# Global/local attention, MoE and soft MoE on one core: two H pieces of tile 1 taken from beside attention of batch 0 to beside the joint softmax chain of tiles 2 and 0

## The chip, the cores and the metric

The kernel runs on one core of one Trainium2 chip. The metric is device time in microseconds (us) of one execution; times below are medians of several runs unless a single execution is named.

## What is computed

The reference, cut to its structure (4 batches, 8 heads, 512 local and 32 global positions, head width 64; model width 512, hidden width 2048; 8 soft-MoE experts with 4 slots each):

```
out_l = softmax([q_l k_g^T, band(q_l k_l^T, 32)] / 8) [v_g; v_l]     per batch and head
out_g = softmax(q_g [k_g; k_l]^T / 8) [v_g; v_l]
x = concat(out_g, out_l)                     rows x 512
h = x @ w_in;  g = max(0.01 h, h);  y = g @ w_out
logits = y @ phi;  d = softmax over rows;  c = softmax over slots
slot_in = d^T y;  slot_out = per expert relu(slot_in w1) w2
result = c @ slot_out
```

w_in and w_out come as 64-bit words and are turned into float32 on the chip.

## The kernel before

The local rows are cut into 16 row tiles of 128 (tile t is part t % 4 of batch t // 4); tile 16 holds the global rows. The kernel works through attention batch by batch and head pair by head pair, and through the row tiles beside it.

**Attention of one head pair n.** T_ (L390 to L406) transposes keys and queries on TensorE, ScalarE evicts them (L394), VectorE builds key windows `kw` (L405, L406). a_S forms scores `sc` on TensorE (L434), VectorE adds the mask and takes the maximum (L446), ScalarE takes the exponentials `se` (L454). a_E transposes them (L473), a_V multiplies by the values `vw` (`po`, L493) and VectorE scales the product (L501). g_S, g_E and g_V do the same for the 32 global queries (`gl` L519, `gs` L536, `get` L561, `gpo` L579, `gxt` L592).

**A row tile t.** b_X transposes the tile and splits it into a high and a low part (`xxh`, `xxl`; tile 2 uses the buffers `qn`, `kn` of the attention and is named `xqn`, `xkn`). b_H(t, f), here called H(t,f), is one of four pieces: 12 matmuls of 512 columns into `hp` (L689) and one Prelu on ScalarE (L696), for hidden columns 512 f to 512 f + 511. A tile needs all four. b_L transposes the hidden tile (`gtp`, L726; copies L728), p_M multiplies by `pmat` to logits `lg` (L887), and p_D1 to p_D3 and u_add run the column softmax and the weighted sum `up` (L810). Tiles 2 and 0 go through this joint softmax chain as one pair, then tiles 1 and 3 (pair_items).

**w_out.** p_items takes w_out in 16 chunks of 128 rows, c0 to c15 here. Each is loaded (`rraw` and, for the first ones, `sraw`, `eraw`, `kraw`, L233), converted by two ScalarE instructions (L251, L250), two on VectorE (L253, L257) and one on GpSimd (L261), stored to DRAM as `wo_f` (L338), transposed on TensorE (`wotp`, L345), evicted by ScalarE (L347) and multiplied with phi (`ptps`, L354). Three `wo` buffers and a ring of four raw buffers tie the chunks to each other: chunk k+3 overwrites the buffer of chunk k, and the load of chunk k+4 waits until GpSimd has ended chunk k. All loads and stores named here are issued in order by SyncE's one queue.

**Order of the work.** The program writes work items with a weight each, `merge` interleaves two lists in proportion to their weights, and a scheduler then fixes the order on each engine, which the chip follows. So one order per engine is fixed before the run.

Before the change, H(0..2, f) run in the order tile 0, 1, 2 for each f: f = 0 and 1 beside the conversion of w_in, f = 2 and 3 beside the first w_out chunks. Then the attention of batch 1 and the other chunks follow with H(3,0), H(3,1), and then the pair chains.

Of the kernel before, what the change touches and what calls it, by code (L numbers as in the profile page):

```python
# [20 lines left out]
def kernel(  # L21
# [24 lines left out]
    NQ = FF // 512  # L46
# [18 lines left out]
    def hb(name):  # L65
        return bank("hb", name, 2)
# [550 lines left out]
    def load_ahead(n):  # L617
        if n < len(order):
            load_qk(*order[n])
# [8 lines left out]
    def step(n):  # L628

        b, i = order[n]  # L630
        last = i == NP - 1
        e = (0.9, lambda: a_E(b, i))
        v = (1.6, lambda: (a_V(b, i), None if n < NP else load_vn(b) if i == NP - 2 else load_v(n + (1 if last else 2))))
        ns = [(2.7, lambda: a_S(*order[n + 1]))] if n + 1 < NN else []
        nt = [(0.9, lambda: T_(n + 2))] if n + 2 < NN else []
        if not last:
            gs = [(2.2, lambda: g_S(b))] if i == NP - 2 else []
            return ns + [e] + gs + nt + [v]
        gv = (2.1, lambda: (g_V(b), load_v(n + 2) if b else None))
        return [e, (0, lambda: None), v, (1.1, lambda: g_E(b))] + ns + nt + [gv]  # L640
# [33 lines left out]
    def b_H(t, f, half=None):  # L674
        xh, xl = xt[t]
        if half != 1:
            if f == 0:
                gt[t] = (
                    xa.tile([P, FF], F32, tag="xn", name="gx", bufs=1) if t in (3, NTT - 1)
                    else sa.tile([P, FF], F32, tag="vw", name="g2", bufs=2) if t == 2  # L680
                    else sb.tile([P, FF], F32, tag="g", name="g", bufs=2)
                )
            hps[0] = hb("hp")
        hp = hps[0]
        w = wi[f]
        lo, hi = {None: (0, KD), 0: (0, KD // 2), 1: (KD // 2, KD)}[half]
        for k in range(lo, hi):
            for n, (a, c) in enumerate(((xh, 0), (xh, 1), (xl, 0))):
                nc.tensor.matmul(  # L689
                    hp, a[:, k, :], w[c][:, k, :],  # L690
                    start=(k == 0 and n == 0), stop=(k == KD - 1 and n == 2),
                )
        if half == 0:
            return
        gs = gt[t][:, 512 * f:512 * f + 512]
        nc.scalar.activation(out=gs, in_=hp, func=AF.Prelu, alpha=0.01)  # L696
        if t in BLK or t in HALF and f < 2:
            blocks(t, f, gs)
# [3 lines left out]
    def blocks(t, f, gs):  # L702

        if f % 2 == 0:
            gbl[0] = sb.tile([P, 2, 512], F32, tag="gT", name="gb", bufs=2)
            gbl[1] = gp[0].tile([P, 2, 4, P], F32, tag="g8", name="g8", bufs=2)
        gb, g8 = gbl[0], gbl[1]
        nc.vector.transpose(out=gb[:, f % 2], in_=gs)  # L708
        lst[t, f] = g8[:, f % 2]
        if f % 2 == 0:  # L710
            return
        src = gb.rearrange("p f (q c j) -> p (f q) c j", c=4, j=32)
        dst = g8.rearrange("p f q (a j) -> p (f q) a j", j=32)
        for n in range(16):
            a, c = n // 4, (n + n // 4) % 4
            copy = {"P": nc.gpsimd.tensor_copy, "A": nc.scalar.copy, "D": nc.vector.tensor_copy}[MOVE[f // 2][n]]
            copy(dst[32 * c:32 * c + 32, :, a], src[32 * a:32 * a + 32, :, c])  # L717
# [3 lines left out]
    def b_L(t, f, ev=None):  # L721
        g = gt[t]
        pt = tp("gtp")
        for c in range(4):
            o = 512 * f + P * c
            nc.tensor.transpose(pt[:, P * c:P * c + P], g[:, o:o + P], ident)  # L726
        gT = part("gT")
        (ev or (nc.vector.tensor_copy if f % 2 and not (t >= 6 and f in (1, 3, 9)) else nc.scalar.copy))(  # L728
            gT, pt
        )  # L730
        lst[t, f] = gT.rearrange("p (c t) -> p c t", c=4)
# [71 lines left out]
    def u_add(ds, last):  # L803

        up = bank("po", "up", 1) if last >= 7 else hb("up")
        later = "u" in ms
        ms["u"] = True
        for n, (d, g) in enumerate(ds):
            for j in range(4):
                ms["up"] = nc.tensor.matmul(  # L810
                    up[32 * j:32 * j + 32, :], d, g[:, 512 * j:512 * j + 512],
                    start=(n == 0), stop=(n == len(ds) - 1), skip_group_check=True,
                ).ins
        if later:
            nc.vector.scalar_tensor_tensor(
                out=uacc, in0=uacc, scalar=ms["al"], in1=up, op0=ALU.mult, op1=ALU.add
            )
        else:
            nc.vector.tensor_copy(uacc, up)
# [59 lines left out]
    def p_M(ts, i):  # L879

        if i == 0:
            ms["M"] = bank("sm", "lg", 1)
        lg = ms["M"]
        for f in range(NQ):
            gT = lst.pop((ts[i], f))
            for c in range(4):
                nc.tensor.matmul(  # L887
                    lg[32 * c:32 * c + 32, P * i:P * i + P], pmat[:, c, f, :], gT[:, c, :],
                    start=(f == 0), stop=(f == NQ - 1), skip_group_check=True,
                )  # L890

    def p_D1(ts):
        lp = sb.tile([P, 2 * P], F32, tag="lp", name="lp", bufs=1)
        nc.vector.tensor_copy(lp, ms["M"][:, 0:2 * P])
        ms["lp"] = lp

    def p_D2(ts):
        ms["st"] = d_cols(ms["M"][:, 2 * P:4 * P], ms["lp"])

    def p_D3(ts):  # L900
        lg = ms["M"]
        for i, t in enumerate(ts):
            nc.tensor.transpose(lg[:, P * i:P * i + P], ms["st"][:, P * i:P * i + P], ident)
        ms["ds"] = [(d_rows(t, lg[:, P * i:P * i + 64]), gt.pop(t)) for i, t in enumerate(ts)]

    def pair_items(ts):
        its = []
        for i, t in enumerate(ts):
            its += [
                (0.9, lambda t=t: (b_L(t, 0), b_L(t, 1))),  # L910
                (0.9, lambda t=t: (b_L(t, 2), b_L(t, 3))),
                (0.6, lambda i=i: p_M(ts, i)),
            ]
        return its + [
            (0.1, lambda: p_D1(ts)),
            (0.5, lambda: p_D2(ts)),
            (0.5, lambda: p_D3(ts)),
            (2.0, lambda: u_add(ms["ds"], ts[-1])),
        ]
# [36 lines left out]
    def merge(a, c):  # L956
        ta, tb = sum(x[0] for x in a) or 1.0, sum(x[0] for x in c) or 1.0
        pa = pb = 0.0
        a, c = list(a), list(c)
        while a or c:  # L960
            if a and (not c or pa / ta <= pb / tb):
                w, f = a.pop(0)[:2]
                pa += w
            else:
                w, f = c.pop(0)[:2]
                pb += w
            f()
# [6 lines left out]
    t = wp.tile([P, 4, NT, 2, D], F32, tag="w", name="qk")  # L974
# [36 lines left out]
        conv(4)  # L1011
    load_ahead(NP)
    load_ahead(NP + 1)
    hs = [[(2.6, lambda t=t, f=f: b_H(t, f)) for t in range(3)] for f in range(NQ)]
    with tc.issue_after(exp_last[0]):
        conv(4)
        merge(hs[1], wit[:4])
# [8 lines left out]
    s4, s5, s6, s7 = (step(n) for n in range(NP, 2 * NP))  # L1026
    h3 = [(2.6, lambda f=f: b_H(3, f)) for f in range(NQ)]
# [4 lines left out]
    xb.append(bctx.enter_context(tc.tile_pool(name="xb", bufs=1, side="right")))  # L1032
    gctx = ExitStack()
    gp.append(gctx.enter_context(tc.tile_pool(name="gp", bufs=1, side="right")))
    merge(pair_items((2, 0)), [h3[2]] + s5[:1])
    load_v(NP + 1)
    merge(h3[3:] + pair_items((1, 3)), s4[-1:] + s5[1:] + s6 + s7)
    b_X(NT)
# [342 lines left out]
```

## Time and profile before

| | us |
|---|---|
| median of 3 runs | 499.89 |
| lowest, highest run | 499.71, 501.77 |
| the profiled execution | 496.2 |
| span of that execution, first to last instruction | 494.5 |
| TensorE busy in the span | 463.5 (94%) |
| VectorE, ScalarE, GpSimd busy | 275.0, 234.3, 160.3 |
| granted TensorE clock, mean | 0.979 |

Busy time of TensorE contains the tail of each matmul, so matmuls that wait one after the other for small results still look nearly dense. All times of the trace are counted from the first instruction of the span; the stretch around the change is 85 to 185 us.

### The profile page before, as it was taken

How to read it: one execution, taken by the hardware profiler on the slowest of the kernel's cores; microseconds unless marked ns; L12 is line 12 of the kernel's file. 1: busy time of each engine (PE TensorE's matmuls, PEld its weight loads, DVE VectorE, ACT ScalarE, POOL GpSimd, SP SyncE). 2: the span in 40 equal slices, each digit the busy share in tenths (PEclk: the TensorE clock that was granted, in tenths of full speed). 3: DMA queues.
4: the chain of work that ended last, by engine and by line, in shares of the span. 5: the costliest groups of instructions: out<-in, count | busy, mean ns of one | idle time of the engine just before them, and what ended most of it. 6: DMA issues, size and time to landing. Idle time of an engine off the chain costs nothing.

```text
span 494.5 us, 13438 instructions
## 1 busy us (share of the span) xinstructions
PE 463.5 (94%) x5323; PEld 322.0 (65%) x5323; DVE 275.0 (56%) x886; ACT 234.3 (47%) x680; POOL 160.3 (32%) x281
## 2 busy tenths in 40 slices
PE   7867889999989999999999999999999999999993
PEld 5645668666766657776777676777777777533463
DVE  4585888498547776556554656427666511413332
ACT  4776899588655345543435444234444432201122
POOL 2044887342400113460615243243667700000000
PEclk9986899999999999999999999999999999999998
DMA  9989598599457655334250231169420079999977
GB/s 177 223 200 267 183 292 313 185 304 311 150 143 144 143 118 93 85 76 129 60 106 1 60 60 45 44 220 405 150 78 2 23 266 357 364 397 371 305 237 214
DMA packets 118362, 90.23 MB, mean 182 GB/s; under 512 B 75356, under 2 KB 100764, under 8 KB 118300
## 3 DMA queue, kind: packets, MB, share of 16 engines
q1 hardware_dynamic: 115628, 88.33, 61.8%
q10 hardware_dynamic: 2672, 1.05, 0.8%
q8 instruction: 42, 0.69, 0.6%
q14 instruction: 20, 0.16, 0.1%
HBM read 76.68 MB, written 8.65 MB: 173 GB/s over the span
## 4 chain that ended last, share of the span: by engine, by line
PE 78%; DVE 4%; ACT 4%; DMA 1%; issue 1%; POOL 0%; ACTq 0%; DVEq 0%; POOLq 0%
PE hp L689 38%; PE gtp L726 4%; PE ehp L1221 3%; PE sc L434 3%; PE up L810 3%; PE po L493 3%; PE lg L740 2%; PE etp L473 2%; PE sop L1297 2%; PE sop L1275 1%; PE gpo L579 1%; PE wotp L345 1%; PE qTp L390 1%; PE kTp L390 1%; PE xtp L659 1%; PE gl L519 1%
## 5 line engine op out<-in xcount | busy, mean ns | idle before, releaser
L689 PE MATMUL hp<-wi,xxh 128*128 128x512 f32 x512 | 167.2, 408 | 1.2 <-ACT xxh L665 1.2
L689 PEld LDWEIGHTS hp<-wi,xxh 128*128 128x128 f32 x512 | 91.8, 190 | 28.2 <-issue 8.2
L717 POOL COPY g<-gb 32x256 f32<-32x256 f32 x206 | 82.7, 401 | 82.6 <-DVE gb L708 55.5
L689 PE MATMUL hp<-wi,xxl 128*128 128x512 f32 x256 | 101.0, 396 | 0.0
L696 ACT ACTIVATE g<-hp 128x512 f32<-128x512 f32 x60 | 35.3, 595 | 56.2 <-PE hp L689 54.2
L454 ACT ACTIVATE se<-se,nmx 128x128 f32<-128x128 f32 x128 | 49.6, 390 | 21.5 <-DVE nmx L452 21.4
L689 PEld LDWEIGHTS hp<-wi,xxl 128*128 128x128 f32 x256 | 48.3, 189 | 12.5 <-issue 1.7
L200 POOL COPY vw<-vw 32x1664 f32<-32x1664 f32 x10 | 15.8, 1575 | 78.3 <-DMA vw<-in_v_g_dram 34.9
L446 DVE CUSTOM_DVE_ANT_0 se<-sc,mask 128x128 f32<-128x128 f32 x128 | 28.9, 284 | 12.1 <-PE sc L434 12.0
L261 POOL TENSOR_TENSOR wn<-wn,rraw 128x512 int32<-128x512 int32 x16 | 22.8, 1435 | 34.5 <-DVE wn L257 33.0
L708 DVE STREAM_TRANSPOSE gb<-g 128x512 f32<-128x512 f32 x32 | 22.2, 702 | 19.3 <-ACT g L696 14.0
L434 PE MATMUL sc<-kw,qT 64*32 64x128 f32 x1024 | 29.2, 283 | 0.8 <-DVE mx L446 0.4
L493 PE MATMUL po<-vw,eT 128*32 128x64 f32 x1024 | 24.2, 232 | 3.5 <-issue 2.1
L261 POOL TENSOR_TENSOR wo<-wo,rraw 128x512 int32<-128x512 int32 x12 | 16.0, 1332 | 31.7 <-DVE wo L257 7.2
L434 PEld LDWEIGHTS sc<-kw,qT 64*32 64x32 f32 x1024 | 19.8, 109 | 8.9 <-issue 5.3
L493 PEld LDWEIGHTS po<-vw,eT 128*32 128x32 f32 x1024 | 18.4, 116 | 10.2 <-issue 7.4
L477 DVE COPY eT<-etp 128x512 f32<-128x512 f32 x28 | 18.7, 684 | 9.9 <-PE etp L473 9.9
L454 ACT ACTIVATION_READ_ACCUMULATOR se<-se,nmx 128x1 f32 x128 | 24.1, 188 | 0.0
L473 PE MATMUL etp<-identr,se 128*128 128x128 f32 x128 | 22.4, 296 | 0.2
L405 DVE COPY kw<-kT 128x672 f32<-128x672 f32 x32 | 19.8, 653 | 3.1 <-ACT kT L394 2.7
L251 ACT ACTIVATE rraw<-rraw 128x512 int32<-128x512 uint32 x28 | 18.7, 673 | 4.3 <-DMA rraw<-in_moe_w_out_dram 3.1
L473 PEld LDWEIGHTS etp<-identr,se 128*128 128x128 f32 x128 | 15.8, 146 | 6.3 <-ACT se L454 2.3
(232 smaller groups left out, 777.9 us busy)
## 6 DMA issues: line engine op xcount, KB each, us to landing
ew<-in_moe_w_dram SPq DMA_DIRECT2D x23, 1024.0 KB, 9.5
rraw<-in_moe_w_in_dram SPq DMA_DIRECT2D x16, 512.0 KB, 5.5
vw<-in_v_l_dram SPq DMA_DIRECT2D x60, 112.0 KB, 3.2
rraw<-in_moe_w_out_dram SPq DMA_DIRECT2D x12, 512.0 KB, 6.7
ew<-in_moe_w_dram SPq DMA_DIRECT2D x9, 512.0 KB, 9.2
ew<-in_moe_w_dram SPq DMA_DIRECT2D x17, 256.0 KB, 5.5
wo_f<-wo SPq DMA_DIRECT2D x16, 256.0 KB, 3.2
vn<-in_v_l_dram SPq DMA_DIRECT2D x4, 1024.0 KB, 6.3
```

The lines of the kernel that those rows point to most:

```text
L261: nc.gpsimd.tensor_tensor(out=di, in0=di, in1=m, op=ALU.add)
L405: nc.vector.tensor_copy(kw[:, :, 0:96], src)
L434: last_a[0] = nc.tensor.matmul(bks[e][32 * u:32 * u + 32, P * T:P * T + P], qt[64 * e:64 * e + 64, 32 * U:32 * U + 32], kw[win(U) // (NW / ...
L446: nc.vector.tensor_tensor_reduce(out=s[:, T, :], in0=bk[:, P * T:P * T + P], in1=mask[:, 0 if T == 0 else 2 if T == NT - 1 else 1, :], sca ...
L454: exp_last[0] = nc.scalar.activation(out=s[:, T, :], in_=s[:, T, :], func=AF.Exp, bias=nmx[:, e, T:T + 1], accum_out=sm[:, T, e:e + 1],).ins
L473: last_a[0] = nc.tensor.transpose(pt[:, P * T:P * T + P], es[e][:, T, :], ident).ins
L493: last_a[0] = nc.tensor.matmul(pov[32 * u:32 * u + 32, T, e, :], ets[e][:, 32 * U:32 * U + 32], vw[:, win(U), e, :], start=True, stop=True ...
L689: nc.tensor.matmul(hp, a[:, k, :], w[c][:, k, :], start=(k == 0 and n == 0), stop=(k == KD - 1 and n == 2),)
L696: nc.scalar.activation(out=gs, in_=hp, func=AF.Prelu, alpha=0.01)
L708: nc.vector.transpose(out=gb[:, f % 2], in_=gs)
L717: copy(dst[32 * c:32 * c + 32, :, a], src[32 * a:32 * a + 32, :, c])
L726: nc.tensor.transpose(pt[:, P * c:P * c + P], g[:, o:o + P], ident)
```

## The change

For f = 2 and 3 only tiles 2 and 0 stay in the first list, tile 2 first. H(1,2) and H(1,3) form a new list `h1`, which is put with H(3,2) and one item of head pair 5 beside pair_items((2, 0)).

```
-    hs = [[(2.6, lambda t=t, f=f: b_H(t, f)) for t in range(3)] for f in range(NQ)]
+    hs = [[(2.6, lambda t=t, f=f: b_H(t, f)) for t in ((0, 1, 2) if f < 2 else (2, 0))] for f in range(NQ)]
+    h1 = [(2.6, lambda f=f: b_H(1, f)) for f in range(2, NQ)]
...
-    merge(pair_items((2, 0)), [h3[2]] + s5[:1])
+    merge(pair_items((2, 0)), h1[:1] + s5[:1] + h1[1:] + [h3[2]])
```

No instruction is added or taken away. What the scheduler makes of it on the engines is shown at three places.

TensorE from the transposes of chunk c1 on, after the first 11 matmuls of H(0,3); names are as above. Before:

```order
L345 MATMUL wotp<-identr,wo 128x128 x4
L354 MATMUL ptps<-wt,phis 32x128
L519 MATMUL gl<-kT,qgT 32x512 x4
L689 MATMUL hp<-wi,xxl 128x512
L689 MATMUL hp<-wi,xxh 128x512 x2
L689 MATMUL hp<-wi,xxl 128x512
```

And with the change:

```order
L345 MATMUL wotp<-identr,wo 128x128 x4
L354 MATMUL ptps<-wt,phis 32x128
L519 MATMUL gl<-kT,qgT 32x512 x4
L689 MATMUL hp<-wi,xxl 128x512
L345 MATMUL wotp<-identr,wo 128x128 x4
L354 MATMUL ptps<-wt,phis 32x128
L345 MATMUL wotp<-identr,wo 128x128 x4
L354 MATMUL ptps<-wt,phis 32x128
L519 MATMUL gl<-kT,qgT 32x512 x4
L561 MATMUL get<-identr,gs 128x128 x4
```

Before, the 24 matmuls of H(1,3) and H(2,3) follow, with c2 and c3 after 12 of them each; now c2 and c3 follow at once, and no H piece comes until H(3,0).

SyncE's queue, from the first stores of converted chunks on. Before:

```order
L338 DMA wo_f<-wo 128x512 x5
L233 DMA rraw<-in_moe_w_out_dram 128x1024
L206 DMA vn<-in_v_l_dram 128x8x256
L211 DMA vg<-in_v_g_dram 32x8x64
L338 DMA wo_f<-wo 128x512
L162 DMA kn<-in_k_l_dram 128x4x64 x2
L162 DMA qn<-in_q_l_dram 128x4x64 x2
L233 DMA rraw<-in_moe_w_out_dram 128x1024
```

And with the change:

```order
L338 DMA wo_f<-wo 128x512 x3
L162 DMA qn<-in_q_l_dram 128x4x64
L162 DMA kn<-in_k_l_dram 128x4x64 x2
L162 DMA qn<-in_q_l_dram 128x4x64
L338 DMA wo_f<-wo 128x512 x2
L233 DMA rraw<-in_moe_w_out_dram 128x1024
L206 DMA vn<-in_v_l_dram 128x8x256
L338 DMA wo_f<-wo 128x512
```

The four loads of keys and queries of head pair 5 (into the buffers that tile 2 used) stand ahead of the stores of c3 and c4 and of the load of c8, where they stood behind them.

TensorE between chunks c14 and c15 (tile 1 is `xxh_832`, tile 3 `xxh_1780` before and `xxh_1745` now). Before:

```order
L345 MATMUL wotp_1812<-identr_66,wo_1768 128x128 x4
L354 MATMUL ptps_1839<-wt_1752,phis_152 32x128
L493 MATMUL po_2116<-vw_1494,eT_1759 32x64 x3
L493 MATMUL po_2116<-vw_1494,eT_1766 32x64 x4
L434 MATMUL sc1_1982<-kw_1874,qT_1872 32x128 x8
L434 MATMUL sc1_1982<-kw_1877,qT_1872 32x128 x8
L345 MATMUL wotp_1819<-identr_66,wo_1805 128x128 x4
```

And with the change, from the end of H(1,2) on:

```order
L689 MATMUL hp_1879<-wi_945,xxl_833 128x512
L434 MATMUL sc0_1927<-kw_1846,qT_1844 32x128 x7
L345 MATMUL wotp_1784<-identr_66,wo_1749 128x128 x4
L354 MATMUL ptps_1811<-wt_1738,phis_152 32x128
L434 MATMUL sc0_1927<-kw_1846,qT_1844 32x128
L434 MATMUL sc0_1927<-kw_1849,qT_1844 32x128 x8
L689 MATMUL hp_2009<-wi_1005,xxh_832 128x512
L689 MATMUL hp_2009<-wi_1006,xxh_832 128x512
L689 MATMUL hp_2009<-wi_1005,xxl_833 128x512
```

H(1,2) and H(1,3) come to stand around c14, that is ahead of the pair chain's logits. H(3,2), which ran before c13, goes to where H(3,3) was (between the two halves of `up` of tiles 2 and 0), and H(3,3) goes between the `gl` matmuls of batch 1. From 182 us of the trace before on, the order on TensorE is the same in both.

## Rows read from the trace of the kernel before

**Rows 1.** The page: busy time of TensorE; granted clock in 40 slices.

```profile
PE 463.5 (94%) x5323; PEld 322.0 (65%) x5323; DVE 275.0 (56%) x886; ACT 234.3 (47%) x680; POOL 160.3 (32%) x281
PEclk9986899999999999999999999999999999999998
```

**Rows 2.** Busy us by engine (instructions), granted clock, DMA share, GB/s, by stretch.

```profile
85.00:90.00 5.00, 5.00 (x29) 3.21 (x28) 2.51 (x8) 2.94 (x7) 1.63 (x3) 1.00 0.28 106
90.00:95.00 5.00, 5.00 (x25) 3.61 (x23) 1.61 (x3) 2.55 (x7) 1.30 (x1) 1.00 0.39 115
...
110.00:115.00 5.00, 3.79 (x54) 2.41 (x56) 4.67 (x22) 3.57 (x13) 2.40 (x2) 1.00 1.14 320
115.00:120.00 5.00, 4.75 (x77) 3.34 (x78) 4.46 (x16) 3.74 (x12) 1.31 (x1) 1.00 1.07 272
```

**Rows 3.** Timeline of TensorE: start, length, line, tiles, count [idle before].

```profile
88.60 0.50 PE L689 MATMUL hp<-wi,xxl 128*128 128x512 f32 x1
...
99.32 0.66 PE L345 MATMUL wotp<-identr,wo 128*128 128x128 f32 x4
99.90 0.54 PE L579 MATMUL gpo<-vn,get 128*32 128x64 f32 x24
...
104.37 0.60 PE L390 MATMUL kTp<-identr,kn 128*128 128x128 f32 x4
...
118.22 1.08 PE L434 MATMUL sc<-kw,qT 64*32 64x128 f32 x32
119.23 1.19 PE L689 MATMUL hp<-wi,xxh 128*128 128x512 f32 x4
...
137.36 0.66 PE L345 MATMUL wotp<-identr,wo 128*128 128x128 f32 x4
...
141.05 0.66 PE L726 MATMUL gtp<-identr,g 128*128 128x128 f32 x4 [1.30 <-DVE gT L728]
...
142.72 0.66 PE L726 MATMUL gtp<-identr,g 128*128 128x128 f32 x4
```

**Rows 4.** Chain that ended last: H matmuls of tile 3.

```profile
121.29 4.58 PE hp L689 x20
```

**Rows 5.** Timeline of GpSimd: ends of the conversions of c4, c8, c15.

```profile
90.81 1.30 POOL L261 TENSOR_TENSOR wo<-wo,rraw 128x512 int32<-128x512 int32 x1 [2.38 <-ACT gs L536]
...
105.94 1.33 POOL L261 TENSOR_TENSOR wo<-wo,rraw 128x512 int32<-128x512 int32 x1 [1.33 <-PE wotp L345]
...
134.79 1.30 POOL L261 TENSOR_TENSOR wo<-wo,rraw 128x512 int32<-128x512 int32 x1 [2.25 <-DVE wo L257]
```

**Rows 6.** Timeline of SyncE's queue: loads of c8, `vn`, and keys of pair 5.

```profile
92.55 0.37 SPq L233 DMA_DIRECT2D rraw<-in_moe_w_out_dram  x1
92.98 0.45 SPq L206 DMA_DIRECT2D vn<-in_v_l_dram  x1
...
97.19 1.13 SPq L162 DMA_DIRECT2D kn<-in_k_l_dram  x2
```

**Rows 7.** Timeline of ScalarE: the first conversion step of c8.

```profile
96.49 0.67 ACT L251 ACTIVATE rraw<-rraw 128x512 int32<-128x512 uint32 x1 [2.96 <-DMA rraw<-in_moe_w_out_dram]
```

**Rows 8.** Timeline of VectorE: one small instruction twice.

```profile
117.99 1.32 DVE L459 TENSOR_SCALAR sm<-sm 128x8 f32<-128x8 f32 x1
...
141.11 0.16 DVE L459 TENSOR_SCALAR sm<-sm 128x8 f32<-128x8 f32 x1
```

**Rows 9.** Timeline of TensorE behind the first pair chain.

```profile
166.06 0.66 PE L726 MATMUL gtp<-identr,gx 128*128 128x128 f32 x4 [0.28 <-ACT gs L542]
...
177.43 0.66 PE L561 MATMUL get<-identr,gs 128*128 128x128 f32 x4 [0.98 <-DVE get L563]
```

**Rows 10.** As rows 2, early stretches with gaps on TensorE.

```profile
28.00:32.00 4.00, 1.82 (x66) 1.16 (x59) 2.68 (x12) 2.64 (x5) 1.32 (x2) 1.00 1.14 198
32.00:36.00 4.00, 3.10 (x21) 1.53 (x21) 4.00 (x5) 4.00 (x16) 3.33 (x3) 0.62 0.37 83
...
60.00:64.00 4.00, 2.08 (x12) 1.53 (x10) 2.97 (x5) 3.94 (x9) 3.38 (x4) 1.00 0.73 192
```

## The prediction, made blind

> **What bounds the kernel now.** I read the page first: TensorE is busy 94% of the span [rows 1], so the end moves only if TensorE loses or gains idle time somewhere. The table by stretch then shows two different stages around the change [rows 2]. From 85 to 95 us TensorE is full (5.00 of 5), VectorE is half idle or more (2.51, then 1.61) and the DMA engines carry 0.28 and 0.39 of their time. From 110 to 120 us it is the other way round: VectorE 4.67 and 4.46 of 5, DMA share 1.14 and 1.07, and TensorE has holes (3.79 in 110 to 115). The first stage has matmuls without holes, the second holes without matmuls. That is where a gain could come from: 24 matmuls out of the first stage into holes of a later one.
>
> The timeline of the single engines shows why the stages differ. Chunk c4 of w_out is ready on GpSimd at 92.1 (90.81 + 1.30) [rows 5], but TensorE transposes it at 99.32 [rows 3], because H(1,3) and H(2,3) stand ahead of it.
>
> **The change part by part.** Nothing is added; a piece costs 12 x 4.58 / 20 = 2.75 us of TensorE [rows 4]. The two orders do the same work up to the last matmul of H(0,3), which ends about 88.9 us [rows 3]. From there I go link by link through the new order, with the durations of the trace.
>
> *The chunks.* c2 and c3 are already converted and go at once. c4 does not hang on the moved work: its conversion ends at 92.1 as before [rows 5], so its transposes come near 93.7 instead of 99.32 [rows 3], 5.6 earlier. The load of c8 waits for GpSimd's end of c4, so it issues at 92.55 as before [rows 6], and ScalarE gets it at 96.49 as before [rows 7]. What becomes faster is the order behind it: c5 to c7 no longer wait for H matmuls, so I put the end of c8 near 103 instead of 107.3 (105.94 + 1.33) [rows 5].
>
> *SyncE's queue.* Tile 2's pieces end 2.75 us earlier, so the buffers `qn` and `kn` come free early, and four loads of 128 KB that issued from 97.19 on [rows 6] go near 86 to 88, into a stage where the DMA engines carry 0.28 [rows 2]. They leave the crowded stage, 0.5 MB at its 320 GB/s [rows 2] or 1.6 us of DMA time. I count nothing for it by itself: no engine waits for these four loads directly; it covers the extra pressure of the chunk loads, which come closer together.
>
> *Attention of pair 4.* The global product `gpo` needs `vn`, issued at 92.98 [rows 6] and used at 99.90 [rows 3]; this load doesn't move. So the key transposes that stood at 104.37 [rows 3] gain only about 1.5 us. Behind them the scores gain more, since TensorE no longer alternates them with waits for chunks: the fourth score group, 118.22 before [rows 3], I put near 111.5.
>
> *a_V and H(3,0).* In the new order all of `po` of pair 4 and c12 stand ahead of H(3,0). `po` needs the last exponentials and the evicted transposes. I put the start of H(3,0) near 121, against 119.23 before [rows 3]: nearly 2 us later, with holes on TensorE ahead of it that have no H piece to fill them.
>
> *To c15.* H(3,0) and H(3,1) end near 126.5; then come c13, H(1,2), c14, H(1,3) (5.5 us), eight `gtp` transposes and one score group, and c15's transposes near 134.9. Before it was 137.36 [rows 3]. **Term 1: -2.5 us.** Bounds: at best the whole moved work comes off the front, -5.5; at worst only the later H(3,0) counts, +1.8.
>
> *c15 to the logits.* Before, from c15 to the second tile's first `gtp` at 142.72 there are 5.36 us, with one wait of 1.30 for VectorE's copy `gT` [rows 3]. In the new order the first transposes of tile 2 lie ahead of c13, but a score group (0.5 us, half of the 1.08 of 32 matmuls in rows 3) and ScalarE's exponentials lie in between. I take 5.1. **Term 2: -0.3**, bounds -1.3 (the wait goes entirely) and +0.5.
>
> *What now lies behind.* H(3,2) has the former place of H(3,3), and H(3,3) goes between the `gl` matmuls: **term 3: +2.75**, no bounds, since it is the same 12 matmuls.
>
> *Cover there.* Behind `gl`, TensorE waits 0.28 (twice, one row shown) for the global exponentials and 0.98 for an eviction [rows 9], 1.5 together. H(3,3) gives the first exponential 2.75 us more. **Term 4: -0.9**, between -1.5 and 0 (the second half of `gl` is late by as much).
>
> Sum: -2.5 - 0.3 + 2.75 - 0.9 = -0.95 us, against the profiled execution of 496.2 us, which stands 3.7 under the median of 499.89; on the median 498.9. All best ends: -5.5 - 1.3 + 2.75 - 1.5 = -5.6; all worst: +1.8 + 0.5 + 2.75 = +5.1.
>
> *VectorE beside GpSimd.* A TENSOR_SCALAR of 128x8 took 1.32 us at 117.99, while GpSimd converted a chunk, and 0.16 at 141.11, when GpSimd had nothing [rows 8]. So a conversion can hold up one VectorE instruction for about 1.16. The trace has such stretched instructions in this stage already, and the number of conversions is the same, so I take no difference. The Trainium skill (SBUF — State Buffer, Who interferes with whom) says that the two engines share one port pair as an exclusive lock, so the loser is blocked for the whole instruction; the trace agrees in this row. Taken as a count, with three more conversions falling beside the key windows of pairs 4 and 5, the sum would be about 3.5 us higher, an estimate by that page and rows 8.
>
> **The rivals.**
> *The front really comes off (faster).* If the links that I made slow (a_V ahead of H(3,0), exponentials) run as densely as the moved-away order allows, term 1 is -5.5 and the sum -5.5 - 0.3 + 2.75 - 0.9 = -3.95: 495.9. For it: VectorE and DMA half idle in 85 to 95 [rows 2], with 5 us to be won. Against: the loads of c8 and `vn` issue at the same time as before [rows 6].
>
> *The clock falls (slower).* The new stretch from 89 to 119 has no H piece, so TensorE does small work with holes. After a stretch of that kind, 28 to 32 us with 1.82 busy of 4, the next had a granted clock of 0.62; yet 2.08 busy in 60 to 64 kept 1.00 [rows 10], and so did 3.79 of 5 in 110 to 115 [rows 2]. It decides if a hole as large as that at 28 us opens, most likely where `po` waits near 116. If 10 us of the stretch, with some 6 us of work in it, run at 0.62, that work takes 6 / 0.62 = 9.7: +3.7, sum +2.75, 502.6. The Trainium skill (TensorE: Matmul & The Clock Gate, What's actually happening) says that the array runs at 2.4 GHz only while activity holds the gate open and falls to 1.2 GHz when it has been idle. Rows 10 agree that it falls, but not at every hole.
>
> *The chain is paced elsewhere (slower).* If exponentials and conversions follow ScalarE's and VectorE's own order, H(3,0) starts later, and the moved pieces only queue up behind it: term 1 is +1.8, the sum +1.8 - 0.3 + 2.75 - 0.9 = +3.35, 503.2. For it: VectorE at 4.67 of 5 [rows 2].
>
> *It doesn't do what it says.* In the order, H(1,2) and H(1,3) stand around c14, ahead of the pair chain; what lies beside that chain are H(3,2) and H(3,3). The sum is made on that order, so this needs no chance of its own.
>
> **How the numbers follow.** Forecast 0.49 (alone some 497 to 501.5), front comes off 0.29, clock 0.08, paced elsewhere 0.14. About 0.5%, 2.5 us, is what a measurement of this kernel can tell from no change. Faster by more: the first rival and a small part of the forecast, 0.31. Slower by more: the two slower rivals, most of them, and a little of the forecast, 0.22. Within: 0.47. The range goes from 495.0 (a little under the fast rival) to 503.3 (the slow one); the corners of the all-best and all-worst sums are left out.
>
> **What would show it.** Right: c4's transposes near 94; c8's load still at 92.5; four `kn`/`qn` loads before 90; H(3,0) near 121; c15 near 135; holes on TensorE of 3 us or more in 89 to 119; granted clock 1.00 throughout. Wrong: c15 before 132 (the front came off), a clock below 0.9 between 90 and 125, or c15 after 137. From the second pair chain on the distance between the two traces should stay constant to the end; if it doesn't, something behind 185 us, which I count at nothing because the order there is unchanged, was in play.

## The result, and the profile after

The changed kernel takes 506.39 us (median of 5 runs, 502.95 to 507.14) against 501.29 for the kernel before in the same session. One run of the kernel before was slow (864.57); the other four have a median of 500.59, and against them the ratio is 1.012, 95% interval 1.0087 to 1.0153. The change costs about 6 us where 1 us of gain was forecast, and 506 lies above the range (495.0 to 503.3). Its profiled execution took 502.95 us with a span of 500.9, which is 6.4 longer than the span before.

The page of the changed kernel, busy time of TensorE and granted clock in 40 slices, answers to [rows 1]:

```profile
PE 465.2 (93%) x5323; PEld 322.1 (64%) x5323; DVE 275.0 (55%) x886; ACT 233.4 (47%) x680; POOL 159.5 (32%) x281
PEclk9976799999999999999999999999999999999998
```

The same work on every engine, 6.4 us more span: what came in is idle time of TensorE. The table by stretch (columns as in [rows 2]) shows where:

```profile
90.00:95.00 5.00, 4.33 (x51) 2.29 (x50) 4.64 (x8) 3.52 (x9) 2.13 (x2) 1.00 0.44 138
95.00:100.00 5.00, 2.70 (x18) 1.63 (x18) 4.33 (x13) 3.31 (x9) 1.75 (x2) 1.00 0.94 319
...
105.00:110.00 5.00, 3.01 (x69) 2.71 (x72) 2.83 (x8) 3.45 (x9) 1.30 (x1) 1.00 1.11 311
110.00:115.00 5.00, 3.64 (x94) 2.99 (x86) 5.00 (x25) 3.76 (x9) 1.29 (x1) 1.00 1.05 284
115.00:120.00 5.00, 3.92 (x38) 2.45 (x30) 4.65 (x24) 5.00 (x24) 1.29 (x1) 1.00 1.05 268
120.00:125.00 5.00, 4.57 (x104) 3.39 (x102) 4.34 (x11) 5.00 (x16) 1.31 (x1) 1.00 1.12 336
```

From 90 to 125 us TensorE is no longer full in any of these stretches, though the clock is 1.00 in all. In 105 to 110 no engine is busy for more than 3.45 of 5 us, while the DMA share is 1.11: there the engines wait for each other and for data. The timeline of TensorE, with the instructions of [rows 3] (the last two rows are a wait of [rows 9] and the first weighted sum of the second tile pair, the third `up`, which stood at 183.36):

```profile
94.81 0.66 PE L345 MATMUL wotp<-identr,wo 128*128 128x128 f32 x4
...
104.56 0.49 PE L390 MATMUL kTp<-identr,kn 128*128 128x128 f32 x3
...
113.36 1.93 PE L434 MATMUL sc<-kw,qT 64*32 64x128 f32 x64
...
123.80 1.20 PE L689 MATMUL hp<-wi,xxh 128*128 128x512 f32 x4
...
139.61 0.60 PE L345 MATMUL wotp<-identr,wo 128*128 128x128 f32 x4
...
183.89 0.66 PE L561 MATMUL get<-identr,gs 128*128 128x128 f32 x4 [0.98 <-DVE get L563]
...
189.83 1.07 PE L810 MATMUL up<-g,d 128*32 128x512 f32 x8
```

c4's transposes come 4.5 us earlier (94.81 for 99.32), 5.3 against c0, nearly the 5.6 of the forecast. The chunks behind it gain too, c8's in the end only 1.5 (106.38 for 107.84). The attention of pair 4 gains nothing: the key transposes stay at 104.56 (104.37), and H(3,0) starts at 123.80 instead of 119.23. The loads of c8 and `vn` go out 0.75 later than in [rows 6], and the four `kn`/`qn` loads did move, from 97.19 to 86.64 and on (SyncE's queue):

```profile
86.64 0.39 SPq L162 DMA_DIRECT2D qn<-in_q_l_dram  x1
87.12 1.06 SPq L162 DMA_DIRECT2D kn<-in_k_l_dram  x2
...
93.31 0.37 SPq L233 DMA_DIRECT2D rraw<-in_moe_w_out_dram  x1
93.73 0.45 SPq L206 DMA_DIRECT2D vn<-in_v_l_dram  x1
```

The waits of TensorE between 88 and 124 us (engine, waiting line, releaser: us in total, times, longest):

```profile
PE wotp L345 <- POOL wo L261: 1.4, 1, 1.4
PE wotp L345 <- ACT wt L347: 1.3, 2, 0.8
PE kTp L390 <- issue: 1.2, 1, 1.2
PE ptps L360 <- DVE pv L359: 1.0, 2, 0.6
PE geg L565 <- DVE gnmx L532: 0.9, 1, 0.9
PE sc L434 <- ACT qT L394: 0.8, 1, 0.8
...
```

With the four smaller ones that are left out here (1.3) they are 7.9 us together, from eight different releasers and one that the profile doesn't show ("issue"); the kernel before has 1.3 us of waits up to H(3,0). The two pieces that left took 5.5 us with them, and more than that came back as waits.

### The profile page after: what moved, and what is told of

It is laid out like the page before. It is cut to its first block, busy times and chain, and to the rows that moved or that the text cites. A ratio compares the mean times of both kernels' runs of the same rounds, so it can differ in the third digit from the quotient of the medians.

```text
span 500.9 us, 13432 instructions
## 1 busy us (share of the span) xinstructions
PE 465.2 (93%) x5323; PEld 322.1 (64%) x5323; DVE 275.0 (55%) x886; ACT 233.4 (47%) x680; POOL 159.5 (32%) x281
## 4 chain that ended last, share of the span: by engine, by line
PE 75%; DMA 8%; ACT 5%; DVE 4%; SPq 4%; issue 2%; POOL 0%; ACTq 0%; POOLq 0%; DVEq 0%
PE hp L689 36%; DMA rraw<-in_moe_w_in_dram 4%; PE gtp L726 4%; PE ehp L1222 3%; PE up L810 3%; PE sc L434 3%; PE po L493 2%; PE lg L740 2%; PE etp L473 2%; PE sop L1298 2%; DMA eraw<-in_moe_w_out_dram 1%; PE sop L1276 1%; PE gpo L579 1%; SPq L162 1%; SPq L184 1%
## 5 line engine op out<-in xcount | busy, mean ns | idle before, releaser
L200 POOL COPY vw<-vw 32x1664 f32<-32x1664 f32 x10 | 15.8, 1580 | 86.9 <-DMA vw<-in_v_g_dram 47.6
L708 DVE STREAM_TRANSPOSE gb<-g 128x512 f32<-128x512 f32 x32 | 22.2, 702 | 19.2 <-ACT g L696 13.9
L493 PE MATMUL po<-vw,eT 128*32 128x64 f32 x1024 | 22.1, 224 | 3.1 <-issue 2.6
L493 PEld LDWEIGHTS po<-vw,eT 128*32 128x32 f32 x1024 | 16.9, 111 | 9.5 <-issue 8.1
L405 DVE COPY kw<-kT 128x672 f32<-128x672 f32 x32 | 18.6, 615 | 4.2 <-ACT kT L394 4.1
L1222 PE MATMUL ehp<-ew,siT 128*32 128x512 f32 x128 | 19.3, 596 | 0.4 <-DVE siT L1212 0.4
L728 ACT COPY gT<-gtp 128x512 f32<-128x512 f32 x26 | 14.8, 587 | 10.0 <-PE gtp L726 6.9
```

The lines of the kernel that those rows point to most:

```text
L493: last_a[0] = nc.tensor.matmul(pov[32 * u:32 * u + 32, T, e, :], ets[e][:, 32 * U:32 * U + 32], vw[:, win(U), e, :], start=True, stop=True ...
L1222: nc.tensor.matmul(hp[n][32 * g:32 * g + 32, :], siT[:, k, :], w1x[k, n] if (r, g, k // 2) == (0, 3, 0) else w1t[4 * r + g, k // 2][:, k % ...
```

## Where the time went

c0's transposes come at 81.04 in the one profile and at 81.79 in the other, with as many H matmuls ahead of them; that 0.75 us is of the stage before (see the last section). So I count from c0. "Waits" is TensorE's idle time from c1 to H(3,0), added up from the timeline; the first and the second `up` are the weighted sums of the first tile pair, the third is the first one of the second pair; the end is the span's. The rows that the first line of the table rests on:

```profile
81.04 0.60 PE L345 MATMUL wotp<-identr,wo 128*128 128x128 f32 x4
...
158.74 1.07 PE L810 MATMUL up<-g,d 128*32 128x512 f32 x8
...
183.36 1.07 PE L810 MATMUL up<-g,d 128*32 128x512 f32 x8
```

And of the second line (its third `up` is shown above):

```profile
81.79 0.60 PE L345 MATMUL wotp<-identr,wo 128*128 128x128 f32 x4
...
161.78 1.06 PE L810 MATMUL up<-g,d 128*32 128x512 f32 x8
```

| profiled execution | H(3,0) | waits | first up | second up | third up | end |
|---|---|---|---|---|---|---|
| before | 38.19 | 1.3 | 73.74 | 77.70 | 102.32 | 413.5 |
| change | 42.01 | 7.7 | 76.04 | 79.99 | 108.04 | 419.1 |
| change, second profile (r_after) | 42.29 | 8.0 | 76.31 | 80.26 | 108.30 | 420.6 |
| pieces in both places (e7_both) | 38.17 | 1.4 | 76.32 | 80.28 | 108.33 | 419.6 |
| pieces left out, list of before (e15_drop_again) | 42.15 | 7.7 | 74.78 | 78.73 | 104.38 | 416.7 |
| pieces left out, list of the change (e6_drop_after) | 42.08 | 7.6 | 71.16 | 75.10 | 103.16 | 414.8 |
| tile order only (e3_order201) | 42.19 | 3.2 | 75.20 | 79.16 | 103.78 | 415.1 |
| one more piece in the front (e12_h30_early) | 31.43 | 0.6 | 75.61 | 79.56 | 104.18 | 415.5 |
| lighter conversion, before (e9_light_before) | 36.52 | 0.0 | 71.44 | 75.39 | 100.00 | 414.4 |
| lighter conversion, change (e10_light_after) | 38.29 | 4.8 | 72.32 | 76.26 | 105.35 | 417.6 |
| change, early load of vn (e11_vn_early) | 39.61 | 6.4 | 75.66 | 79.60 | 107.66 | 420.0 |
| change with fill (e8_fill) | 42.73 | 3.5 | 76.83 | 80.78 | 108.82 | 421.1 |

From the third `up` on the change is 5.7 behind and stays so to the end; in its second profile the distance grows to 7.1 there.

H(3,0) and the waits ahead of it are no measure of the loss by themselves, since the work ahead of H(3,0) differs. In the change `po` of pair 4, c12 and some transposes stand ahead of it that stood behind it: its 3.8 us of delay are 6.4 us more of waits, less the 5.5 us of the two pieces, and, as the rest, 2.9 us of such work. From c0 to the second `up`, however, both orders do the same work on TensorE except for H(3,3), which has left this stretch with its 2.75 us. The change still ends the stretch 2.29 later, so 5.0 us came in: nearly all that the two pieces took with them from the front and brought back at their new place. The other 3.43 of the 5.72 arise behind the second `up`, where H(3,3) stands now.

## The experiments

**The first four.** Theories: *holes* (without H pieces TensorE waits in the front, so the pieces lost cover that they had and give nothing back there), *a_V* (the loss is `po` of pair 4 standing ahead of H(3,0)), *queue* (the loss is the four loads of pair 5 standing ahead in SyncE's queue).

One piece only, H(1,3), moved:

```
-  for t in ((0, 1, 2) if f < 2 else (2, 0))
+  for t in ((0, 1, 2) if f < 3 else (2, 0))
-    h1 = [(2.6, lambda f=f: b_H(1, f)) for f in range(2, NQ)]
+    h1 = [(2.6, lambda f=f: b_H(1, f)) for f in range(3, NQ)]
...
-    merge(pair_items((2, 0)), h1[:1] + s5[:1] + h1[1:] + [h3[2]])
+    merge(pair_items((2, 0)), h1 + s5[:1] + [h3[2]])
```

> Only H(1,3) is moved, H(1,2) stays in its old place beside the first w_out chunks. Three theories. Holes: in 89 to 97 us the 24 matmuls lay in time that the chunks and the attention of batch 1 take anyway; taken away they leave holes, and come back later as 5.5 us of work with no hole to go to: half the work, so half the loss, 2 to 4 us slower than before (the change: 6), and the first H piece of tile 3 starts near 121.5 instead of 123.8. a_V: the loss comes from po of pair 4, which the scheduler put ahead of H(3,0): it still stands there in this order, so 5 to 6 us slower. Queue: the loss comes from four loads of keys and queries put ahead of the stores of c3 and c4 and the load of c8: 0 to 2 us slower, since tile 2's last piece now runs later.

504.89 us against 497.62, ratio 1.0143 (1.0106 to 1.0181): a miss, as much as both pieces. Its profile shows a wait that the change does not have, on TensorE:

```profile
122.20 0.30 PE L493 MATMUL po<-vw,eT 128*32 128x64 f32 x4 [2.24 <-DMA rraw<-in_moe_w_out_dram]
```

A second one of 1.00 follows at 123.51, for a load of values. The order of the loads came out differently, and the granted clock falls to 0.71 behind these waits, so this run tells nothing of half the dose.

Both pieces inside the thin stretch, behind the scores of pairs 4 and 5:

```
-  (2.7, lambda: a_S(*order[NP])), (0.9, lambda: T_(NP + 1))
-    ] + s4[:2] + ...
+  (2.7, lambda: a_S(*order[NP])), held(h1[0]), (0.9, lambda: T_(NP + 1))
+    ] + s4[:1] + [held(h1[1])] + s4[1:2] + ...
...
-    merge(pair_items((2, 0)), h1[:1] + s5[:1] + h1[1:] + [h3[2]])
+    merge(pair_items((2, 0)), [h3[2]] + s5[:1])
```

> As the change, but H(1,2) is held behind the scores of head pair 4 and H(1,3) behind those of pair 5, in the stretch from 105 to 120 us of the change's trace, where TensorE was busy 3.0 to 3.9 of 5. Holes: most of the 5.5 us disappears in those holes: within 1.5 us of before, on either side. a_V: po still stands ahead of H(3,0), so 5 to 6 us slower than before. Queue: the loads stand as in the change, 5 to 6 us slower.

505.70, ratio 1.0159 (1.0134 to 1.0183): a miss as well. TensorE's stretches and its H matmuls:

```profile
115.00:120.00 5.00, 3.51 (x19) 2.16 (x17) 3.46 (x18) 3.61 (x18) 1.28 (x1) 0.96 1.05 264
120.00:125.00 5.00, 4.51 (x70) 3.12 (x69) 2.67 (x13) 3.71 (x10) 0.22 (x1) 0.50 1.08 249
```

```profile
124.94 1.22 PE L689 MATMUL hp<-wi,xxh 128*128 128x512 f32 x2
```

The granted clock falls to 0.50 near 120 us, the lower of its two levels (1.2 instead of 2.4 GHz), and two matmuls of H(1,3) take 1.22 us where they take 0.62 elsewhere. The Trainium skill (TensorE: Matmul & The Clock Gate, What's actually happening) describes these two levels; the 0.50 agrees. So this run mixes the place with the clock and doesn't settle the place.

Nothing moved out, only the tile order 2, 0, 1 for f = 2 and 3:

```
-  for t in range(3)
+  for t in ((0, 1, 2) if f < 2 else (2, 0, 1))
```

> No piece is moved out; only the order of tiles for pieces 2 and 3 is 2, 0, 1 instead of 0, 1, 2, so that the buffers for keys and queries of pair 5 come free some 5 us earlier than before. Holes: no piece leaves the front, so within 1 us of before. a_V: part of po ahead of H(3,0), 0 to 2 us slower. Queue: the early loads cost here too, 2 to 5 us slower.

499.46, ratio 1.0047 (1.0023 to 1.0071): some 2 us slower, more than holes gave and less than queue did. The tile order, which frees `qn` and `kn` early, brings no gain by itself: its third `up` comes 1.5 late, against 5.7 in the change. Its H(3,0) comes as late as in the change (42.19) with every piece still in the front, another sign that H(3,0) does not measure the loss.

The change, with `po` of pair 4 held behind H(3,1):

```
-    merge(h3[3:] + pair_items((1, 3)), s4[-1:] + ...
+    merge(h3[3:] + pair_items((1, 3)), [behind_h(s4[-1])] + ...
```

> The change, with a_V of pair 4 held behind H(3,1) (it runs near c15). Holes: the same holes, the work behind them only reordered: 4 to 6 us slower than before; H(3,0) starts 1 to 1.5 us earlier than in the change. a_V: 0 to 2 us slower than before. Queue: 5 to 6 us slower.

504.16, ratio 1.014 (1.0101 to 1.018). The a_V theory falls: with `po` behind H(3,1) nothing of the loss comes back. (The profile has a clock of 0.64 to 0.69 in 100 to 105 and in 115 to 125 us, so its stretches can't be set beside those of the change.)

**What a piece costs in each place.** From here on the theories are *cover* (the holes theory made sharp: a piece costs nothing in the front and its full time at the new place), *work* (2.75 us wherever it stands), *clock* (the loss is a fall of the granted clock) and *order* (the order of the new front is what loses).

Before, without the two pieces; the same edit in e6_drop_after on the change:

```
+    if t == 1 and f >= 2:
+        nc.scalar.copy(gs, gt[t][:, 0:512])
+        return
...
-        for k in range(lo, hi):
+        for k in range(lo, hi if hp is not None else lo):
```

> The kernel before with the 24 matmuls of H(1,2) and H(1,3) left out (the hidden columns 1024 to 2047 of tile 1 are copied from its first 512 by ScalarE instead). Cover theory (in the front TensorE waits for the chunks of w_out anyway, so the two pieces cost next to nothing there): 0 to 1.5 us under before, c15 less than 1.5 us earlier. Work theory (a piece costs its 2.75 us wherever it stands): 5.5 us under before, c15 5.5 earlier.

499.89 against 497.43, ratio 1.0054 (1.0022 to 1.0087). With 24 matmuls fewer the kernel is 2.5 us slower: work falls, and cover, which gave 0 to 1.5 less, misses too. The profiled execution had a clock of 0.56 to 0.76 from 115 to 125 us, hence a second profile:

> A second profile of the kernel before without the 24 matmuls of H(1,2) and H(1,3) (hidden columns of tile 1 copied instead), whose first profile had a granted clock of 0.76 and 0.56 from 115 to 125 us. Cover theory: with the clock at 1.00 there, the third up comes within 1.5 us of its 102.3 behind c0. Work theory: 5.5 earlier than that.

500.29 us in one run, clock 1.00 from 85 to 190 us. H(3,0) lies 42.15 behind c0, as in the change, and the third `up` 104.38, 2.06 later than before (limit of the expectation: 1.5). A wait on VectorE right at that `up`, which the kernel before does not have, is 0.97 of it; of the rest no run shows the cause:

```profile
186.17 1.06 PE L813 MATMUL up<-g,d 128*32 128x512 f32 x8 [0.97 <-DVE d L790]
```

The pieces in both places, which is the change with the old first list:

```
-  for t in ((0, 1, 2) if f < 2 else (2, 0))
+  for t in range(3)
...
     merge(pair_items((2, 0)), h1[:1] + s5[:1] + h1[1:] + [h3[2]])
```

> H(1,2) and H(1,3) are computed twice: in the front as before, and again beside the joint softmax chain as with the change. Cover theory: as the change, within 1.5 us, that is some 6 us over before. Work theory: 5.5 us over the change, since the front is as full as before. Clock theory (the loss of the change is a granted clock that falls in the stretch without H pieces): the full front does not reach into the stretch of 105 to 125 us, so the drop there is as with the change, and the time 3 to 5.5 over it.

502.86 against 497.43, ratio 1.011 (1.0069 to 1.0151). It computes 24 matmuls more than the change and is not slower than it. TensorE's waits between 88 and 124 us, and its third `up`:

```profile
PE wotp L345 <- POOL wo L261: 0.8, 1, 0.8
PE sc L434 <- DVE mx L446: 0.4, 1, 0.4
PE ptps L354 <- ACT wt L347: 0.2, 1, 0.2
```

```profile
189.82 1.06 PE L810 MATMUL up<-g,d 128*32 128x512 f32 x8
```

The change had 7.9 us of waits and reached this instruction at 189.83. With the pieces 1.4 us of waits, without them 7.9, the same end: in the front the pieces stand in time that TensorE waits through otherwise.

The change once more, beside e5 and e7:

> The changed kernel once more, as the yardstick of the other runs of this job and for a second profile. Both theories: 503 to 507. Clock theory: this execution shows a granted clock under 0.9 somewhere between 95 and 130 us if it is slower than the first profiled one (502.95), 1.00 if it is not; cover theory: the third up lies 25 to 26 us behind H(1,3)'s place, 6 us later than before against c0, whatever the clock.

503.92, ratio 1.0127 (1.0089 to 1.0166), granted clock 1.00 from 80 to 145 us. The profiled execution took 504.29. The clock theory falls for the change: no drop in this stretch in either profile, and the same loss. The third `up` is 6.0 later than before against c0, as cover gave.

The change with fill; `fill(4)` stands five times in the list, behind the transposes and the scores of pairs 4 and 5 and behind the transposes of pair 4's exponentials:

```
+    def fill(n):
+        def go():
+            if not fb:
+                fb.append(hb("wm"))
+            for _ in range(n):
+                warm(fb[0])
+        return held((0, go))
```

> The changed kernel with 20 more matmuls of 128x512 on the identity (results unused), in groups of four behind the transposes and scores of pairs 4 and 5, in the stretch that has no H piece. Cover theory (there TensorE waits for the small work of the pairs, so the fill lies in its holes): within 1 us of the change. Clock theory: 2 to 4 us under the change, granted clock 1.00 from 95 to 130. Work theory: 4 to 5 us over the change.

505.76, ratio 1.0151 (1.0101 to 1.0201), 1.8 over the change's median, with intervals that overlap; cover had allowed 1. Its 20 matmuls are 4.6 us of work by [rows 4], the third `up` comes 0.8 later than in the change: most of the fill lies in holes. That speaks for cover, and the missing gain speaks against clock (though a clock of 0.66 from 100 to 105 us stands in its profile).

The change without the pieces at their new place:

> The changed kernel with the 24 matmuls of H(1,2) and H(1,3) left out at their new place (the hidden columns 1024 to 2047 of tile 1 are copied from its first 512 by ScalarE). Cover theory (the two pieces cost nothing in the front and their full 5.5 us at the new place, so the loss of the change is their own time): 5 to 6.5 us under the change, at the level of the kernel before or up to 1 us over it. Order theory (the order of the front without the pieces is itself what loses): within 2 us of the change.

499.54 against 498.09, ratio 1.0036 (1.0013 to 1.006). The third `up`:

```profile
185.91 1.07 PE L813 MATMUL up<-g,d 128*32 128x512 f32 x8
```

That is 103.16 behind c0, 4.9 earlier than with the pieces and 0.8 later than before. In time it is 4.4 under the change's 503.92, measured in another session, where 5 to 6.5 was expected; the order theory (within 2) falls. At the new place the pieces cost 4.9 (e6 to change) and 6.0 (before to e7); their own time is 5.5. Taking them out of the front gives nothing back: the third `up` of the kernels without them is 0.8 (e6) and 2.1 (e15) later than before, not 5.5 earlier. The 0.8 of e6 is hardly of the front, since 0.7 of it arises behind the second `up` (see term 3 below).

**What holds the front.** *Pace* (the conversion chain of a chunk), *load* (`vn`) and *attention* (pair 4's own chain).

```
-        nc.scalar.activation(out=m, in_=lo, func=AF.Copy, scale=2.0 ** -29)
+        if not (wide and half is None):
+            nc.scalar.activation(out=m, in_=lo, func=AF.Copy, scale=2.0 ** -29)
...
+        if wide and half is None:
+            return dst
         di = dst.bitcast(I32)
```

> The kernel before, with a lighter conversion of w_out's chunks c4 to c15: the low word of each 64-bit weight is left out there (no L251 on ScalarE and no L261 on GpSimd, 12 instructions of 0.67 and of 1.30 us). It is the yardstick of the next run. Pace theory (the front goes at the pace of the conversion chain of a chunk): TensorE is still full of H pieces until 99 us, so at most 3 us under before. Attention theory (the front goes at the pace of pair 4's own chain: global part, transposes, scores, exponentials): within 1.5 us of before.

> The changed kernel with the same lighter conversion. Pace theory: with the chain shortened the front is now free to move up, H(3,0) comes 3 us or more earlier than in the changed kernel, and the distance to the yardstick with the same conversion falls from 6 to 3 us or less. Attention theory: the distance stays between 5 and 7.

Before: 497.01, ratio 0.9985 (0.996 to 1.0011). Change: 501.81, ratio 1.0064 (1.0039 to 1.0089). The distance falls from 6.5 to 4.8, which neither theory had. H(3,0) of the change does come 3.7 earlier (38.29 for 42.01), as the pace theory says, and the load of `vn` shows up as a wait of 1.2. At the second `up` 1.4 us more is left than the yardstick gained (3.7 for 2.3), at the third only 0.4 (2.7 for 2.3): a wait of 0.96 on VectorE stands there, as in e15.

```
-    with tc.issue_after(raw_last[0]):
-        load_vn(0)
+    load_vn(0)
```

> The changed kernel with the load of the values of the global product (vn, vg) free of its place behind the load of c8, so it goes out before the w_out chunks. Load theory (gpo, and behind it the transposes of pair 4, wait for this load): gpo 3 us earlier against c0, the whole 2 to 3 us under the change. Pace and attention theories: gpo within 1 us of its place, the time within 1 us of the change, or above it by the crowding of the earlier queue.

505.38, ratio 1.014 (1.0119 to 1.016). `gpo` comes 4.5 earlier against c0 (14.33 for 18.83) and H(3,0) 2.4, as the load theory says; but the second and the third `up` come only 0.4 earlier, and the time doesn't fall, where that theory gave 2 to 3 us. Both reliefs together:

> The changed kernel with both reliefs of the front together: the lighter conversion of c4 to c15 (the low words of w_out left out there) and the early load of vn and vg. Two-chain theory (conversion chain and load of vn are the two paths that hold the front, each hidden by the other): H(3,0) 36 us or less behind c0 (42 in the changed kernel, 38.3 with the lighter conversion alone), and 3 us or less over the yardstick with the same reliefs. Many-chains theory (the softmax steps of pairs 4 and 5 on VectorE and ScalarE are next): H(3,0) still 37.5 or more behind c0, 4 to 6 us over the yardstick.

> The kernel before with the same two reliefs, the yardstick of the run above. Both theories: TensorE is full of H pieces to 99 us, so within 1.5 us of the kernel before.

Before with both: 498.95, ratio 1.0008 (0.9971 to 1.0045). Change with both: 511.05, ratio 1.0243 (1.0192 to 1.0294), a miss for both theories: one wait of 2.8 for exponentials and a clock that falls twice.

```profile
95.00:100.00 5.00, 4.41 (x68) 3.01 (x67) 3.95 (x12) 2.09 (x6) 0.00 (x0) 0.50 0.90 308
...
115.00:120.00 5.00, 4.74 (x54) 2.97 (x55) 4.00 (x23) 4.20 (x19) 0.00 (x0) 0.50 0.97 261
```

With the clock at 0.50 in two stretches this run doesn't show what both reliefs are worth. So neither relief alone gives back more than 1.4 us at the second `up` (1.7 by the times of two sessions), and which links hold the front together stays open.

**More work into the front.** Before, with tile 3's transposes and H(3,0) further ahead in the list; on TensorE H(3,0) then comes behind the scores of pair 4:

```
-    ] + s4[:2] + [(0.5, lambda: b_X(3))] + h3[:2] + s4[2:-1])
+    ] + s4[:1] + [(0.5, lambda: b_X(3))] + h3[:1] + s4[1:2] + h3[1:2] + s4[2:-1])
```

> The kernel before, with one more piece in the front instead of two fewer: the transposes of tile 3 and H(3,0) stand directly behind the scores of pair 4. Cover theory (work in the front lies in waits): H(3,1) ends 1 to 2 us earlier than before against c0, the time 0.5 to 2 us under before. Work theory: no change, within 0.5; if the piece delays the chain of pair 4, up to 2 us over before.

499.68, ratio 1.0019 (0.9997 to 1.0041), no gain: a miss for cover. H(3,0) starts 6.8 earlier and the waits fall to 0.6, but the third `up` is 1.9 late. The profile has a hole at 135 to 140 us (3.88 of 5 busy) and a clock of 0.51 behind it; that pair 4's chain, pushed back behind the piece, makes that hole is my reading and not shown. The front before had 1.3 us of waits, so there was little to fill. No version beat the kernel before (the lighter conversion, 0.9985, can't be told from it).

## Why the prediction was wrong

**The reading "matmuls without holes" was the failing step.** The first part read 85 to 95 us as a stage that TensorE alone sets, because it was full there [rows 2], and term 1 rests on it. TensorE was full because the pieces filled it. Beneath them ran work of the other engines and two loads that takes as long without the pieces (e6, e15), which [rows 5 to 7] showed in part: the loads of c8 and `vn` at the same times, ScalarE waiting 2.96 for c8. The prediction wrote these times down as unchanged and still let the links behind them come earlier. In the chain that ended last, the stretch from 88 to 97 us of the kernel before is TensorE alone, most of it H matmuls, like these:

```profile
88.67 3.18 PE hp L689 x13
```

In the changed kernel it is (a part of it, in order of time):

```profile
91.55 1.58 DVE wo L253
...
94.45 0.07 DVE wo L253
94.52 1.14 issue
...
106.72 3.71 DMA kn<-in_k_l_dram
...
114.47 2.73 ACT se L454 x14
...
123.87 1.13 PE hp L689 x4
```

It goes through VectorE and the exponentials of pairs 4 and 5 on ScalarE; H matmuls come back at 123.87. The load of keys is doubtful: the conversion step that it is said to release reads no keys, and VectorE was at work until then. In the second profile the chain has no such load, but this one, of c8:

```profile
93.31 3.75 DMA rraw<-in_moe_w_out_dram
```

**Term 1: -2.5, measured +2.25 for c15 (137.36 to 139.61), 1.5 of it behind c0.** This is the largest part of the miss: behind c0 the sum was -0.95 and the third `up` came 5.72 late, and of the 6.7 us between them 4.0 lie in term 1, 1.1 in term 2 and 1.6 in terms 3 and 4. Link by link: c4 near 93.7 was nearly right (94.81, of which 0.75 is c0's). The end of c8 was put near 103 and came at 104.86 (103.56 + 1.30 on GpSimd). The key transposes should gain 1.5 and gained 0.56 against c0. The fourth score group was put near 111.5; the third and fourth now run in one row, from 113.36 to 115.29, so the fourth began near 114.3. H(3,0) was put near 121 and came at 123.80. From there to c15 I had 13.9 and it took 15.8: H(3,0) and H(3,1) took 6.15 instead of 5.5, the two moved pieces 5.8 instead of 5.5, and the chunks, transposes and scores between them 3.9 instead of 2.9. The worst bound of +1.8 held for c15 behind c0, but not for H(3,0), which it was made on: 3.8 later, with 6.4 us more of waits ahead of it.

**VectorE beside GpSimd: taken as no difference, right as a sum, but not in its place.** VectorE in the changed kernel:

```profile
91.55 1.57 DVE L253 TENSOR_SCALAR wo<-wo 128x512 uint32<-128x512 uint32 x1 [0.33 <-ACT wo L250]
...
94.37 1.37 DVE L253 TENSOR_SCALAR wo<-wo 128x512 uint32<-128x512 uint32 x1
```

Both stand beside GpSimd's conversions of c4 and c5 (91.54 and 94.17, 1.3 us each), and both are on the chain above, the second as 0.07 and the 1.14 of "issue" behind it. The kernel before has 0.43 for one of these at 93.56, with GpSimd idle, and without GpSimd's step (e10) the second looks like this:

```profile
95.04 0.42 DVE L254 TENSOR_SCALAR wo<-wo 128x512 uint32<-128x512 uint32 x1
```

So these two took 2.1 us more than they do alone (1.57 + 1.37 less twice 0.42). The Trainium skill (SBUF — State Buffer, Who interferes with whom) has the loser blocked for the whole instruction; these rows agree, each ending 0.28 behind GpSimd's. But the kernel before has stretched instructions too, later, besides the one in [rows 8]:

```profile
103.63 1.26 DVE L253 TENSOR_SCALAR wo<-wo 128x512 uint32<-128x512 uint32 x1
...
105.64 2.04 DVE L405 COPY kw<-kT 128x672 f32<-128x672 f32 x2
...
112.67 1.28 DVE L406 COPY kw<-kgT 128x224 f32<-128x224 f32 x1
```

Counted as what each takes above the shortest of its kind, from c0 to 42 us behind it, they come to 4.1 us before and 4.1 in the change. So "no difference" was right, and the second count (3.5 more) was not. What the prediction did not ask is where the stretched ones fall: two of them now stand at 91.55 and 94.37, in the part that the H matmuls had hidden. What that costs by itself no run settled.

**Term 2: -0.3.** From c15 to the first `up` it took 18.22 instead of 17.42, so +0.8, over the worst bound of +0.5. The score group now behind c15 took 1.0 (140.47 to 141.48) where I had 0.5, and the waits there stayed: 1.58 for 1.64.

**Term 3: +2.75, right in kind, and term 4: -0.9, measured 0.** From the second `up` of the first pair to the third it takes 28.05 (189.83 less 161.78) for 24.62 before, +3.43 for both terms together. All three waits of [rows 9] are there in full, 0.28 twice and 0.98: H(3,3) stands ahead of the second half of `gl`, whose results are waited for, and pushes both back; the prediction named this case as the upper bound of term 4. The 0.68 beyond the piece's 2.75 is mainly `gl` itself. Before, its 16 matmuls ran in one go:

```profile
160.76 1.09 PE L519 MATMUL gl<-kT,qgT 64*32 64x512 f32 x16
```

Now H(3,3) splits them, and each part takes about as long as the whole did:

```profile
163.79 1.07 PE L519 MATMUL gl<-kT,qgT 64*32 64x512 f32 x10
...
168.62 1.06 PE L519 MATMUL gl<-kT,qgT 64*32 64x512 f32 x6
```

From start to next start these are 1.02 before and 1.00 + 0.98 now, 0.96 more; the `lg` matmuls behind, which now run in one go and not in two, give 0.3 of it back. Term 3 had no bounds "since it is the same 12 matmuls"; what they split was not asked.

**The rivals.** "The chain is paced elsewhere" was the case that came (chance 0.14), with a price too low (503.2). Its term 1 of +1.8 was near the +1.5 measured behind c0; what it lacks lies in terms 2 to 4, +1.55 together where +4.2 came. "The clock falls" did not happen here in either profile of the change, but did between 95 and 145 us in those of e1, e2, e4, e5, e8, e12, e13 and e14, with the old front and with the new, and may add to the scatter of their times. "The front really comes off" is excluded by e6, e7 and e15. Of the signs named for a wrong forecast, c15 after 137 came; the clock of 1.00 from 80 to 145 us came as named, and so did the constant distance behind 185 us in the first profile of the change.

## What to carry to other kernels

An engine that is 5.00 of 5 busy in a stretch is not thereby what sets its end. Before moving independent work out of such a stretch, take away that work in thought and follow the other engines' chain with its own in-order waits; if that is about as long, the work is free where it is and costs its full time anywhere that is dense. One kernel with the work in both places, and one with it in neither, show the price of each place directly. Compare two orders at a point ahead of which both have done the same work: H(3,0) was 3.8 to 4.0 us late in the change, in e6 and in e3 alike, whose third `up` came 5.7, 0.8 and 1.5 late.

## What the runs showed of the hardware

The stage ahead of the change is not the same from one execution to the next. e5 and e15 are the same kernel, and yet c0's transposes came at 84.14 and at 81.79 us; among the kernels with as many H matmuls ahead of c0 the range goes from 81.04 (before) to 84.44 (e8). The granted clock from 60 to 70 us differs too: it was 1.00 in the profiles of the kernel before and of the change, and 0.83 in those of e2, e8 and e15. It doesn't explain the shift alone, since e15 has c0 as early as the change. So differences of 3 us between two single executions can come from there, and the tables above count from c0.

The 16 `gl` matmuls (64x512) took 1.02 us when they followed each other directly, and 1.00 and 0.98 when H(3,3) split them in 10 and 6: without other matmuls between them their two parts overlap.
